# Attention and gated MLP block on one core: program order from the wo stage on, its large GpSimd work on VectorE

## The chip, the core and the metric

The kernel runs on one core of a Trainium2 chip. A core has five queues that work side by side and wait for one another through semaphores: TensorE (PE in the profile, with its weight loads as PEld), VectorE (DVE), ScalarE (ACT), GpSimd (POOL) and SyncE (SP), which here issues nearly all DMAs. The metric is the device time of one execution in microseconds; the time before is the median of 3 runs.

## The reference

One transformer block on x of 2048 tokens by 640, in float32, without learned scales:

```python
# A: 32 heads of 20, each token sees itself and the 255 before it
qkv = layernorm(x) @ wqkv
p = softmax(where(mask, q @ k.T * 20**-0.5, -1e9))
h = x + (p @ v) @ wo
# B: F = 1728, Fh = 864
z = gelu(layernorm(h) @ w_in)
z1, z2 = z[:, :Fh], layernorm(z[:, Fh:])
g = w_sp @ z2 + b_sp[:, None]          # w_sp is 2048 x 2048, over tokens
out = h + (z1 * g) @ w_out
```

## The kernel before

Tokens lie in 16 tiles of 128. Every float32 operand of a large product is split in two parts: hi, a rounded copy (made by ScalarE), and lo, the difference raw - hi (a two-input subtraction). A product is hi x hi + hi x lo + lo x hi, three TensorE instructions. Some products also use a scheme with seven block products in place of eight: the seven left blocks and seven right blocks (B11, T1, T2, B22, T3, B21, T4) are sums and differences of quarters, each with its own hi and lo.

The stages, in order of time:

1. LayerNorm, v and q, k (to about 190 us), then attention (to about 488 us). Attention runs over 130 steps `s`, four heads at a time: in step s, scores of unit u = s, its exponentials on ScalarE, and the product with v (`pv_item`) of unit s - 2. Each odd unit copies half of its output bank to `ot` (on ScalarE or VectorE, line 397) and SyncE stores that to `o_d`; a later pv product in the same bank waits for the copy. The row sums go with it: `inverse_sums(c)` loads them again, takes the reciprocal on VectorE and stores it to `r_d`. It is a generator: each `yield` puts the rest one step later. So is `proj_early`, which in the last 16 steps loads wo and splits it (lines 180 and 181), loads two pairs of token tiles of the output (`load_o`: five DMAs and the reciprocals), multiplies (`norm_o`) and splits (`split_o`) tiles 0 and 1. `proj_o(0)` and `proj_o(1)`, the product with wo, run in the last two steps.
2. The wo stage (to about 583 us): a loop over the 16 tiles. For each: `norm_o` and `split_o` of a later tile, `proj_o` (30 TensorE instructions), h = x + product, store to `h_d`, LayerNorm, transposes (`turn_h`) and a store of the transposed tile to `hn_d`. Beside it, `win1_prep` makes the right blocks of w_in's first half, and the first left blocks of stage 3 are prepared.
3. z1 (to about 668 us): `z_pair`, 8 pairs of tiles, 8 steps each.
4. z2 for 8 tiles (to about 716 us): `z2_pair`, four pairs of tiles. Each is four steps (t, h), a row tile t by a half h: 15 products into a bank (tag `a`, four banks), then a gelu on ScalarE into the row `z[t]`. Then come the statistics of the row (`stat`: two bn_stats and an aggregate on VectorE, three operations of one column on GpSimd), `norm` (scaling on ScalarE), and `right_blocks` of the pair, which the gates use as right operand.
5. `first_gate`, 8 pairs (to about 856 us): products of w_sp with these rows; the partial result goes to `g_d`.
6. z2 for the other 8 tiles (to about 904 us), then `second_gate`: the second half of w_sp, plus g_d, times z1, transposed (`turn_y`) and multiplied by w_out (`project`). In the first of these pairs w_out is loaded tile by tile into two buffers and split (`put_wout`).

From stage 3 on the program is a list `steps`, each a TensorE part and an evacuation, and a table `later`: `at(n, f)` puts f ahead of step n. `run(n)` writes first all of `later[n]`, in the order in which they were put there, then the step's product, then its evacuation:

```python
def run(n):
    for f in later.pop(n, []):
        f()
    if 0 <= n < len(steps):
        steps[n][0]()
        steps[n][1]()
```

Events of a pair are put there when the pair is written, pair after pair. At n0 + 4, the first step of the next pair, stand the older pair's `stat(1, 1)`, `norm(1)` and fourth part of the right blocks, then the new pair's lo of tile t = 1 (at n0 of the new pair).

What sets the order on the queues: up to line 626 `manual_schedule` is in force, which keeps TensorE, VectorE, ScalarE and SyncE in the order in which the program writes its instructions. `ms.close()` there ends it. From then on a scheduler orders the instructions by its own model, with what the program wrote as a start; it can also place later instructions among earlier ones, as it did with three loads of x and one of w_in that SyncE issues at 452 to 456 us. GpSimd is under the scheduler throughout.

Of the kernel before, what the change touches and what calls it, by code (L numbers as in the profile page):

```python
# [15 lines left out]
P = 128  # L16
# [18 lines left out]
def block_kernel(ctx, tc, x, wqk, wv, wo, w_in, wsp, bsp, w_out, out):  # L35
# [45 lines left out]

    def gemm(ps, n, lhs, rhs, ks):
# [61 lines left out]
    def norm_o(i, eng):  # L144
        ot, rs = ots[i]
        eng.tensor_tensor(out=ot, in0=ot, in1=rs[:, None, :].to_broadcast([P, KD, P]), op=OP.mult)

    def split_o(i, eng):
        ot, _ = ots[i]
        osp = mem["osp2"] if i % 3 == 2 else t1((2 * KD + i % 3 * 2) * D, 2, KD, P)  # L150
        if eng is nc.vector:
            eng.tensor_copy(out=osp[:, 0], in_=ot)
        else:
            nc.scalar.activation(osp[:, 0], ot, AF.Copy)
        eng.tensor_tensor(out=osp[:, 1], in0=ot, in1=osp[:, 0].bitcast(F32), op=OP.subtract)
        ots[i] = osp

# [7 lines left out]
    def proj_early():  # L165
# [12 lines left out]
        for k in range(KD):  # L178
# [3 lines left out]
            if k in (1, 3):  # L182
                yield
        yield
        rs = load_o(0)
        yield
        yield
        rs()
        yield
        yield  # L190
        load_o(1)()
        yield
        for i in range(2):
            norm_o(i, nc.vector)
            split_o(i, nc.vector)
            yield


    with ExitStack() as ab:
# [132 lines left out]
        def inverse_sums(c):  # L332
# [8 lines left out]
            yield  # L341
            nc.vector.reciprocal(out=t, in_=t)
# [28 lines left out]
        def pv_item(u):  # L371
# [20 lines left out]
            if kb % 2:  # L392
# [4 lines left out]
                if u >= NU - 5 or j == 0 and u < NU - LEAD:  # L397
# [183 lines left out]
        for s in range(NU + 2):  # L581
# [5 lines left out]
            for hh in range(4):  # L587
# [9 lines left out]
                if hh == 2 + s - NU and s >= NU:  # L597
                    if s == NU:
                        psB.close()
                        psW = pool(psB, "psW", space=PSUM)  # L600
                    pre_ps.append(proj_o(s - NU, psW.tile([P, 2, 512], F32, tag="wo", bufs=3, name=f"wo_ps{s - NU}")))
                if s >= 2:
# [3 lines left out]
                    if hh == 3:  # L606
                        next(pv, None)
            if u1 == NU:
# [17 lines left out]
    ms.close()  # L626
# [78 lines left out]
    def win1_prep(raw):  # L705
        seven, last = win1
        src = w_in[:, :FH].rearrange("k (h c) -> k h c", h=2)
        for k in range(2):
# [5 lines left out]
            for f in right_blocks(lambda: [s[k] for s in seven], *(raw[:, b, h] for b in range(2) for h in range(2)),  # L714
                                  eng=nc.gpsimd):
# [9 lines left out]
    def win2_prep(raw):  # L725
        for k in range(KD):
# [5 lines left out]
            minus(win2[0][:, 1, k], raw, win2[0][:, 0, k].bitcast(F32), nc.gpsimd)  # L732
# [33 lines left out]
    def turn_h(i):  # L766
        ht = mem["ho"][i % 3]
        if i < NT - 2:
# [99 lines left out]
    def z2_pair(q, i, j, k):  # L868
# [6 lines left out]
        def prep(t, first, eng):  # L875
# [3 lines left out]
            else:  # L879
                minus(a[t][:, 1], r3, a[t][:, 0].bitcast(F32), eng)  # L880
# [11 lines left out]
        for t, tile_t in ((0, i), (1, j)):  # L892
# [3 lines left out]
            at(m - (1 if soon else 3), lambda t=t: prep(t, True, None))  # L896
            at(m - (1 if soon else 2), lambda t=t: prep(t, False, nc.gpsimd if t else nc.vector))
# [6 lines left out]
        def stat(t, h):  # L904
# [4 lines left out]
            if h:  # L909
                nc.vector.bn_aggr(out=mv[:, 0:2], in_=st)  # L910
                nc.gpsimd.tensor_scalar(out=mv[:, 2:3], in0=mv[:, 1:2], scalar1=EPS, scalar2=None, op0=OP.add)
                nc.gpsimd.tensor_tensor(out=mv[:, 3:4], in0=mv[:, 2:3], in1=half, op=OP.pow)
                nc.gpsimd.tensor_scalar(out=mv[:, 2:3], in0=mv[:, 0:1], scalar1=mv[:, 3:4], scalar2=-1.0,
                                        op0=OP.mult, op1=OP.mult)

        def norm(t):
            mv = stats[t][1]
            nc.scalar.activation(z[t], z[t], AF.Identity, bias=mv[:, 2:3], scale=mv[:, 3:4])
# [11 lines left out]
    def gate_pair(p, c, post, extra):  # L930
# [13 lines left out]
        eng = nc.vector if p else nc.gpsimd  # L944

# [6 lines left out]
        def s13():  # L952
            plus(s1, a21, a22, eng=eng)
# [267 lines left out]
```

## Time and profile before

| | us |
|---|---|
| median of 3 runs | 1164.73 (1162.14 to 1165.46) |
| the profiled execution | 1165.89 |
| its span, first to last instruction | 1163.7 |
| TensorE busy | 1102.1 |
| VectorE / ScalarE / GpSimd busy | 736.8 / 553.9 / 404.8 |

Times in the profile are microseconds from the span's start. A group of instructions is told by line, engine, operation, the tiles it writes and reads, their shapes and count, then busy time and mean duration of one, then the idle time of the engine just ahead of them and what ended it. `[5.00 <-DVE ot L400]` behind an instruction of the timeline means that its engine was idle for 5.00 us and was released by VectorE's write of `ot` in line 400. SPq is SyncE's queue of DMAs. The lines that carry the argument are shown in the prediction.

### The profile page before, as it was taken

How to read it: one execution, taken by the hardware profiler on the slowest of the kernel's cores; microseconds unless marked ns; L12 is line 12 of the kernel's file. 1: busy time of each engine (PE TensorE's matmuls, PEld its weight loads, DVE VectorE, ACT ScalarE, POOL GpSimd, SP SyncE). 2: the span in 40 equal slices, each digit the busy share in tenths (PEclk: the TensorE clock that was granted, in tenths of full speed). 3: DMA queues.
4: the chain of work that ended last, by engine and by line, in shares of the span. 5: the costliest groups of instructions: out<-in, count | busy, mean ns of one | idle time of the engine just before them, and what ended most of it. 6: DMA issues, size and time to landing. Idle time of an engine off the chain costs nothing.

```text
span 1163.7 us, 28646 instructions
## 1 busy us (share of the span) xinstructions
PE 1102.1 (95%) x11152; PEld 994.7 (85%) x11152; DVE 736.8 (63%) x1961; ACT 553.9 (48%) x1181; POOL 404.8 (35%) x530
## 2 busy tenths in 40 slices
PE   6999999999999999788999998999999799999998
PEld 6998886667877777588999997999999699999998
DVE  5541213788999986679858468655547874655542
ACT  4334433258998889534257566433336531222110
POOL 3124443456666667446421066000117420000000
PEclk9999999999999999889999999999999999999999
DMA  4222355545555543578736512232341454444332
GB/s 149 78 69 80 136 169 201 184 152 176 184 182 176 179 136 125 164 233 270 245 138 210 167 65 73 67 130 87 119 152 39 157 167 152 142 132 143 93 94 68
DMA packets 79800, 165.35 MB, mean 142 GB/s; under 512 B 10752, under 2 KB 43264, under 8 KB 75776
## 3 DMA queue, kind: packets, MB, share of 16 engines
q1 hardware_dynamic: 77360, 158.28, 42.0%
q10 hardware_dynamic: 2304, 5.24, 1.2%
q8 instruction: 87, 1.43, 0.5%
q14 instruction: 49, 0.40, 0.1%
HBM read 108.83 MB, written 54.66 MB: 140 GB/s over the span
## 4 chain that ended last, share of the span: by engine, by line
PE 62%; ACT 8%; issue 7%; POOL 7%; DVE 6%; DMA 6%; SPq 3%; ACTq 0%; POOLq 0%; DVEq 0%
PE g L992 21%; PE out_ps L1057 8%; ACT pt L363 5%; PE pv L386 4%; PE bank L300 3%; PE bank L361 3%; PE zx L835 2%; POOL sg L486 2%; PE zv L835 2%; PE zb L886 2%; PE zy L835 2%; PE zw L835 1%; PE wo_ps L89 1%; PE qk L467 1%; PE qk L468 1%
## 5 line engine op out<-in xcount | busy, mean ns | idle before, releaser
L363 ACT ACTIVATE pt<-bank 128x384 f32<-128x384 f32 (+2 forms) x512 | 202.5, 484 | 29.4 <-PE bank L361 22.3
L992 PE MATMUL g<-zl,aw 128*128 128x432 f32 x768 | 174.4, 363 | 8.8 <-ACT zl L650 8.3
L650 ACT ACTIVATE aw<-fx 128x512 fp32r<-128x512 f32 (+2 forms) x160 | 92.9, 595 | 187.3 <-PE g L992 122.3
L310 DVE CUSTOM_DVE_ANT_0 junk<-bank,strip 128x288 bf16<-128x288 f32 x392 | 156.2, 454 | 15.2 <-PE bank L300 13.8
L992 PEld LDWEIGHTS g<-zl,aw 128*128 128x128 f32 x768 | 145.4, 190 | 17.3 <-ACT zl L650 10.5
L992 PE MATMUL g<-ze,aw 128*128 128x432 f32 x576 | 136.2, 366 | 4.6 <-ACT aw L650 4.5
L386 PE MATMUL pv<-pt,v_sb 128*32 128x192 f32 (+3 forms) x1984 | 130.9, 326 | 10.1 <-DVE ot L400 5.0
L644 DVE TENSOR_TENSOR aw<-fx,aw 128x512 fp32r<-128x512 f32 (+2 forms) x152 | 111.9, 746 | 37.0 <-ACT aw L650 36.3
L992 PEld LDWEIGHTS g<-ze,aw 128*128 128x128 f32 x576 | 109.8, 192 | 10.3 <-ACT aw L650 5.2
L361 PE MATMUL bank<-slot 123*32 123x288 bf16 (+7 forms) x1536 | 110.0, 280 | 2.4 <-issue 1.1
L365 POOL TENSOR_SCALAR_AFFINE_SELECT pt<-pt 128x512 f32<-128x512 f32 x128 | 81.9, 640 | 70.6 <-ACT pt L363 69.3
L1057 PE MATMUL out_ps<-wout,y_sp 128*128 128x320 f32 (+1 forms) x630 | 96.2, 309 | 0.4 <-ACT y_sp L122 0.4
L886 PE MATMUL zb<-win,aw 128*128 128x432 f32 x480 | 95.3, 359 | 0.0
L1057 PEld LDWEIGHTS out_ps<-wout,y_sp 128*128 128x128 f32 (+1 forms) x630 | 94.1, 188 | 1.2 <-ACT y_sp L122 0.7
L886 PEld LDWEIGHTS zb<-win,aw 128*128 128x128 f32 x480 | 89.9, 187 | 4.7
L300 PE MATMUL bank<-slot 120*32 120x288 bf16 (+6 forms) x1280 | 92.2, 277 | 0.9 <-issue 0.8
L483 DVE TENSOR_TENSOR rest<-qk,sg 128x512 f32<-128x512 f32 x40 | 27.7, 692 | 89.5 <-ACT sg L481 89.5
L386 PEld LDWEIGHTS pv<-pt,v_sb 128*32 128x32 f32 x1984 | 61.9, 111 | 17.8 <-issue 14.3
L361 PEld LDWEIGHTS <-slot 123*32 123x32 bf16 x1728 | 60.3, 98 | 17.1 <-issue 8.3
L486 POOL TENSOR_TENSOR sg<-rest,sg 128x512 bf16<-128x512 f32 x40 | 46.5, 1164 | 75.1 <-ACT sg L485 73.2
L368 POOL TENSOR_SCALAR_AFFINE_SELECT pt<-pt 128x512 f32<-128x512 f32 x112 | 71.6, 639 | 0.0
L644 DVE TENSOR_TENSOR row<-g,row 128x432 f32<-128x432 f32 x80 | 48.2, 604 | 36.1 <-PE g L992 32.7
(192 smaller groups left out, 2221.1 us busy)
## 6 DMA issues: line engine op xcount, KB each, us to landing
slot<-qk_d SPq DMA_DIRECT2D x144, 160.0 KB
fx<-wsp_in SPq DMA_DIRECT2D x32, 512.0 KB
qk_d<-sg SPq DMA_DIRECT2D x40, 384.0 KB
fx<-hn_d SPq DMA_DIRECT2D x32, 320.0 KB
o_d<-ot SPq DMA_DIRECT2D x64, 128.0 KB
xb<-qk_d SPq DMA_DIRECT2D x48, 160.0 KB
z_d<-row SPq DMA_DIRECT2D x16, 432.0 KB
g_d<-row SPq DMA_DIRECT2D x16, 432.0 KB
```

Of the source, the lines that this page charges most:

```text
L300: nc.tensor.matmul(ps[32 * j:32 * j + 32, o:o + w], one(st, 120, 0, hh, q0, 32), k, start=True, stop=True, tile_position=(0, 32 * j))
L310: nc.vector.tensor_tensor_reduce(out=junk[:, :n], in0=ps[:, :n], in1=keep, scale=1.0, scalar=NEG, op0=OP.add, op1=OP.max, accum_out=m_cols ...
L361: nc.tensor.matmul(ps[32 * i:32 * i + 32, b + o:b + o + w], one(st, 123, 1, hh, k0, 32), q, start=True, stop=True, tile_position=(0, 32 * i))
L363: nc.scalar.activation(pt[:, hh, :n], ps[:, :n], AF.Exp, scale=SCALE)
L365: nc.gpsimd.affine_select(out=pt[:, :, :P], in_=pt[:, :, :P], pattern=[[0, 4], [1, P]], base=0, channel_multiplier=-1, compare_op=OP.is_ge ...
L386: nc.tensor.matmul(ps[32 * hh:32 * hh + 32, a - 512 * c:b - 512 * c], v_sb[:, kb, v0:v0 + 32], pt[:, hh, a - kb * P:b - kb * P], start=fir ...
L644: (eng or nc.vector).tensor_tensor(out=out, in0=a, in1=b, op=op)
L650: nc.scalar.activation(out, a, AF.Copy)
L835: nc.tensor.matmul(ps, a[x], b[:, y], start=start and m + x + y == 0, stop=stop and m == n - 1 and x == 1, skip_group_check=True)
L886: nc.tensor.matmul(b[0][:, :HF], a[t][:, x, kk], win2[0][:, y, kk, h * HF:(h + 1) * HF], start=kk + x + y == 0, stop=kk == KD - 1 and x == 1)
L992: nc.tensor.matmul(ps, w[m][:, x, k], zc[k][m][:, y], start=start and k + x + y == 0, stop=stop and k == 3 and x == 1, skip_group_check=True)
L1057: nc.tensor.matmul(ps[j][:, :HD], src[:w, a, k, :], e1["wout"][:w, b, k, j * HD:(j + 1) * HD], start=(k == 0 and a + b == 0), stop=(k == K ...
```

## The change

- `ms.close()` is removed, so program order holds to the end for TensorE, VectorE, ScalarE and SyncE.
- Subtractions and sums that went to GpSimd from wo on go to VectorE: split_o's lo, the right blocks of `win1_prep` and of `z2_pair`, win2's lo, the second row tile's lo in `z2_pair`, the preparations of the first pair of either gate, w_out's lo. GpSimd keeps the three one-column operations of each LayerNorm.
- `norm(0)` and the first three parts of the right blocks go from n0 + 2 to n0 + 3.
- The wo loop is written anew, as a pipeline over iterations: in iteration i the product of tile i, `norm_o` and `split_o` of tile i + 1, the sum and the statistics of tile i - 1, its scaling, and the transposes of tile i - 2. LayerNorm's last step moves from VectorE to ScalarE (`scaled`); h_d's store moves from ScalarE's queue to SyncE's. The transposes of tile 14 fall into the loop, that of tile 15 goes to step 2, and what followed it moves one step.
- The end of attention: one split of wo a step where two stood together, `load_o` earlier, the reciprocal one step later, `norm_o(2)` ahead of the loop; the copies of the units 123 to 125 go from ScalarE to VectorE; `proj_o` of the last two steps is written behind the pv of its step.

```diff
+    def stats_of(mv, st):
+        nc.vector.bn_aggr(out=mv[:, 0:2], in_=st)
+        nc.gpsimd.tensor_scalar(out=mv[:, 2:3], in0=mv[:, 1:2], scalar1=EPS, scalar2=None, op0=OP.add)
+        nc.gpsimd.tensor_tensor(out=mv[:, 3:4], in0=mv[:, 2:3], in1=half, op=OP.pow)
+        nc.gpsimd.tensor_scalar(out=mv[:, 2:3], in0=mv[:, 0:1], scalar1=mv[:, 3:4], scalar2=-1.0,
+                                op0=OP.mult, op1=OP.mult)
+
+    def scaled(dst, src, mv):
+        nc.scalar.activation(dst, src, AF.Identity, bias=mv[:, 2:3], scale=mv[:, 3:4])
...
-    def split_o(i, eng):
+    def split_o(i, on_dve=False):
...
-        eng.tensor_tensor(out=osp[:, 1], in0=ot, in1=osp[:, 0].bitcast(F32), op=OP.subtract)
         ots[i] = osp
+        return lambda: nc.vector.tensor_tensor(out=osp[:, 1], in0=ot, in1=osp[:, 0].bitcast(F32), op=OP.subtract)
...
-            if k in (1, 3):
-                yield
+            if k == 2:
+                rs0 = load_o(0)
+            if k == 4:
+                rs1 = load_o(1)
+            yield
+        rs0()
         yield
-        rs = load_o(0)
-        yield
-        yield
-        rs()
-        yield
-        yield
-        load_o(1)()
+        rs1()
         yield
         for i in range(2):
-            norm_o(i, nc.vector)
-            split_o(i, nc.vector)
+            norm_o(i)
+            split_o(i, True)()
             yield
+        norm_o(2)
...
             nc.sync.dma_start(t, rows(o_d[:, DH, c * 512:(c + 1) * 512], 32 * S))
+            yield
             yield
             yield
             nc.vector.reciprocal(out=t, in_=t)
...
-                if u >= NU - 5 or j == 0 and u < NU - LEAD:
+                if u >= NU - 2 or j == 0 and u < NU - LEAD:
...
-    ms.close()
...
-            for f in right_blocks(lambda: [s[k] for s in seven], *(raw[:, b, h] for b in range(2) for h in range(2)),
-                                  eng=nc.gpsimd):
+            for f in right_blocks(lambda: [s[k] for s in seven], *(raw[:, b, h] for b in range(2) for h in range(2))):
...
-            at(m - (1 if soon else 2), lambda t=t: prep(t, False, nc.gpsimd if t else nc.vector))
+            at(m - (1 if soon else 2), lambda t=t: prep(t, False))
...
-        f = right_blocks(lambda: zc[k], *blocks, nc.vector if k == 3 else nc.gpsimd)
+        f = right_blocks(lambda: zc[k], *blocks)
         at(n0 + 1, lambda: stat(0, 0))
-        at(n0 + 2, lambda: (stat(0, 1), norm(0), f[0](), f[1](), f[2]()))
-        at(n0 + 3, lambda: stat(1, 0))
+        at(n0 + 2, lambda: stat(0, 1))
+        at(n0 + 3, lambda: (stat(1, 0), norm(0), f[0](), f[1](), f[2]()))
         at(n0 + 4, lambda: (stat(1, 1), norm(1), f[3]()))
         at(n0 + 5, lambda: (f[4](), f[5](), f[6]()))
...
-        eng = nc.vector if p else nc.gpsimd
...
-                split(e1["wout"][:, 0, k], e1["wout"][:, 1, k], e1["h"][k // 4], nc.gpsimd)
+                split(e1["wout"][:, 0, k], e1["wout"][:, 1, k], e1["h"][k // 4])
...
+    for i in range(1, NT + 1):
+        more = i + 1 < NT
+        if 1 < i < NT:
+            pre_ps.append(proj_o(i, acc_tile(f"wo_ps{i}")))
+        if 1 < i < NT - 1:
+            norm_o(i + 1)
+        if more:
+            lo = split_o(i + 1)
+        if i > 1:
+            add_h(i - 1)
+        if more:
+            lo()
+        if i == 1:
+            add_h(0)
+        if i == 1 or i % 2 == 0 and i + 4 < NT:
             load_o(i // 2 + 2)()
+        for n in (2, 3, 4) if i == 1 else (i + 3,) if i + 3 < NT else ():
             load_x2(n)
+        bn_h(i - 1)
+        next(w1, None)
+        scaled(hn(i - 1), hs.pop(i - 1), stat_h.pop(i - 1)[1])
+        run(i - NT - 1)
         if i > 1:
             turn_h(i - 2)
+        if i % 3 == 1:
             next(w1, None)
```

`add_h(i)` is the sum h = x + product on VectorE and its store; `bn_h(i)` is two bn_stats and `stats_of`.

More of the change, by code (lines that the diff above doesn't have):

```diff
@@ L596, in block_kernel @@
                     next(rows)
[L597 to L601, printed above, removed]
                 if s >= 2:
@@ L607, in block_kernel @@
                         next(pv, None)
+                if hh == 2 + s - NU and s >= NU:
+                    if s == NU:
+                        psB.close()
+                        psW = pool(psB, "psW", space=PSUM)
+                    pre_ps.append(proj_o(s - NU, psW.tile([P, 2, 512], F32, tag="wo", bufs=3, name=f"wo_ps{s - NU}")))
             if u1 == NU:
@@ L731, in win2_prep @@
             yield
[L732 removed]
+            minus(win2[0][:, 1, k], raw, win2[0][:, 0, k].bitcast(F32))
             for _ in range(4):
@@ L873, in z2_pair, with prep @@
         z = [row(), row()]
-        def prep(t, first, eng):
+        def prep(t, first):
             r3 = r[t].rearrange("p (k t) -> p k t", k=KD)
```

63 lines of the change are left out of this document (26 added, 37 removed).

## The prediction

> **What bounds the kernel now.** I read the page first, then the busy time of the engines stage by stage, then TensorE's timeline at each place where it idles, then the queues of the other engines there.
>
> ```profile
> span 1163.7 us, 28646 instructions
> PE 1102.1 (95%) x11152; PEld 994.7 (85%) x11152; DVE 736.8 (63%) x1961; ACT 553.9 (48%) x1181; POOL 404.8 (35%) x530
> 466.00:488.00 22.00, 13.73 (x261) 9.60 (x258) 10.70 (x16) 12.78 (x36) 11.37 (x17) 0.83 0.57 182
> 488.00:583.00 95.00, 86.28 (x569) 83.66 (x569) 80.60 (x132) 30.93 (x55) 49.25 (x52) 0.93 0.72 236
> 583.00:668.00 85.00, 85.00 (x440) 81.22 (x439) 55.03 (x102) 51.61 (x97) 12.68 (x8) 1.00 0.51 176
> 668.00:716.00 48.00, 48.00 (x245) 45.59 (x244) 34.47 (x50) 29.32 (x51) 31.13 (x34) 1.00 0.20 66
> 716.00:734.00 18.00, 13.27 (x51) 11.30 (x50) 14.98 (x28) 12.17 (x23) 6.95 (x10) 0.81 0.14 47
> 904.00:945.00 41.00, 32.42 (x151) 29.49 (x150) 35.14 (x53) 20.61 (x37) 21.24 (x16) 0.92 0.49 166
> ```
>
> Columns of the stages: length; busy time of PE, PEld, DVE, ACT, POOL; granted clock; DMA share; GB/s. TensorE (PE) is the bound. The change can win only its idle time from about 460 us on: 8.3 us at the end of attention (22.00 - 13.73), 8.7 in the wo stage, 4.7 at the entry of the first gates, 8.6 at that of the second, and what the clock loses behind these gaps. The z_pair stage (583 to 668) and the zb products (668 to 716) are at 100%: there is nothing to win there and something to lose.
>
> ```profile
> 471.19 1.08 PE L386 MATMUL pv<-pt,v_sb 128*32 128x256 f32 x8 [5.00 <-DVE ot L400]
> 487.69 5.93 PE L89 MATMUL wo_ps<-t 128*128 128x320 f32 x30 [2.22 <-DVE t L152]
> 498.53 4.56 PE L89 MATMUL wo_ps<-t,osp 128*128 128x320 f32 x30
> 512.27 7.16 PE L89 MATMUL wo_ps<-t 128*128 128x320 f32 x30 [1.55 <-DVE xh L1165]
> 725.51 0.47 PE L992 MATMUL g<-zl,aw 128*128 128x432 f32 x1 [4.40 <-ACT zl L650]
> 729.81 3.08 PE L992 MATMUL g<-ze,aw 128*128 128x432 f32 x8
> 931.25 3.21 PE L992 MATMUL g<-ze,aw 128*128 128x432 f32 x8 [4.49 <-ACT aw L650]
> ```
>
> A gap costs twice: 30 products behind a wait of 2 us take 5.9 to 7.2 us where 4.6 is normal, and 8 gate products take 3.1 us where 0.2 us each is normal. The Trainium skill (TensorE: Matmul & The Clock Gate, Part 1) puts the drop to half clock at about 3.4 us without work; here waits of 1.55 and 2.22 us already lengthen what follows, so the measurement decides.
>
> **The change in the z2 stage, the largest term.** Each pair of rows is four TensorE steps (t,h) of 15 products. Durations:
>
> ```profile
> L886 PE MATMUL zb<-win,aw 128*128 128x432 f32 x237 | 47.1, 359 | 0.0
> L890 ACT ACTIVATE row<-zb 128x432 f32<-128x432 f32 x13 | 6.7, 517 | 1.8 <-PE zb L886 1.8
> L908 DVE BATCH_NORM_STATS2 stz<-row 128x6 f32<-128x432 f32 x13 | 7.7, 590 | 0.6 <-ACT row L890 0.6
> L910 DVE BATCH_NORM_AGGREGATE mvz<-stz 128x2 f32<-128x12 f32 x6 | 1.2, 202 | 0.2
> 723.80 0.22 POOL L911 TENSOR_SCALAR mvz<-mvz 128x1 f32<-128x1 f32 x1
> 724.78 0.27 POOL L913 TENSOR_SCALAR mvz<-mvz 128x1 f32<-128x1 f32 x1
> L918 ACT ACTIVATE row<-row,mvz 128x864 f32<-128x864 f32 x6 | 6.6, 1108 | 9.2 <-POOL mvz L913 9.2
> L650 ACT ACTIVATE zl<-row 128x432 fp32r<-128x432 f32 x6 | 3.2, 558 | 0.3 <-POOL row L644 0.2
> 726.78 1.92 ACT L650 ACTIVATE zl<-row 128x432 fp32r<-128x432 f32 x4 [0.32 <-DVE row L644]
> L650 ACT ACTIVATE aw<-fx 128x640 fp32r<-128x640 f32 x5 | 3.6, 723 | 0.0
> L644 DVE TENSOR_TENSOR zl<-row,zl 128x432 fp32r<-128x432 f32 x7 | 4.0, 604 | 2.9 <-ACT zl L650 2.9
> L644 DVE TENSOR_TENSOR ze<-row,ze 128x432 fp32r<-128x432 f32 x9 | 9.1, 1029 | 3.5 <-ACT ze L650 3.5
> L644 DVE TENSOR_TENSOR aw<-fx,aw 128x640 fp32r<-128x640 f32 x3 | 2.5, 826 | 2.9 <-ACT aw L650 2.9
> ```
>
> In total VectorE gains from the move: a subtraction of 128x432 takes 0.604 us alone and 1.029 while GpSimd works. All of a pair's vector work in the new order is 11 right-block operations x 0.5 (0.604 less the 0.1 by which neighbours overlap: four copies of 0.558 took 1.92), four bn_stats, two aggregates and two "lo" parts of 0.83: about 10.5 us, under TensorE's 60 x 0.199 = 11.9. By sums it fits. But both queues are now written by hand, and they wait for each other. I follow them from the end of one pair's last gelu, gelu(1,1), to that of the next:
>
> - bn_stats, aggregate: 0.9. Three small GpSimd operations: 1.25 (723.80 to 725.05). norm(1), 1.11: ends at 3.4.
> - ScalarE: hi(B21), then hi(T2), which waits for a VectorE difference, then hi(B22); only then gelu(0,0), done at 5.4. VectorE: two differences, then "lo" of the row tile t=1, which was GpSimd's: done at 5.3.
> - VectorE: three lo's and a difference, 7.4. ScalarE: hi(T4), hi of the next tile, gelu(0,1), done at 9.0; gelu(1,0), 9.4.
> - The statistics of row 0 wait for gelu(0,1): 9.9. GpSimd 11.2. norm(0), now behind gelu(1,0): 12.4. hi(B11) 12.9; lo and difference 14.1; hi(T1) 14.7; hi of the next tile 15.3; gelu(1,1) 15.7.
>
> The loop takes 15.7 us for 11.9 us of products (60 x 47.1/237), so the queues lag 3.8 us more per pair. TensorE notices through the "lo" of t=1: its third step waits for it, 5.3 us after the last gelu. The first pair, without a predecessor, ends 1.35 us late, so pair 2 stalls 1.3 us. Pair 3 stalls 4.3 and pair 4 stalls 6.4, because the first gate's preparations (five VectorE operations of 0.6 and four copies of 0.5 in these two loops) stand in the same queues. At the gate, 27 products of three pieces run, then the fourth piece needs B21 of the last row: 5 us behind the last gelu, a stall of 3.0. T2 accumulates in the bank of B11, whose evacuation now stands behind all remaining copies of the last row in ScalarE's queue: 2.5. Sum 17.5, and 1.5 for the clock: 19 us. Today this entry loses 4.7 idle, 2.5 in its window by the clock (19% of 13.27) and some 1.5 after it, say 9. **First z2 stage: +10.** A microsecond more or less in the loop moves the last gelu by three, so the bounds are +14 (a loop of 17 us, while GpSimd's three take longer under VectorE's load) and -5 (no lag: only some 4 us of the entry remain).
>
> Second z2 stage: the same 19, and 2 more, because there the evacuation is VectorE's and stands behind w_out's first lo as well: 21. Today it loses 8.6 idle and 8% of 32.42, 11.2. Six of these are w_out's:
>
> ```profile
> 922.60 4.37 POOL L123 TENSOR_TENSOR wout<-hr,wout 128x640 fp32r<-128x640 f32 x1 [3.87 <-ACT wout L122]
> 929.94 0.74 ACT L122 ACTIVATE wout<-hr 128x640 fp32r<-128x640 f32 x1 [3.39 <-DMA hr<-w_out_in]
> ```
>
> GpSimd holds w_out's buffer for 4.37 us, the next load waits for it on SP, ScalarE waits for the load, and the gate's own copy behind it makes the 4.49 us gap at 931. On VectorE the lo takes 0.83, and that chain goes. 21 - 11.2 = **+10**.
>
> z_pair steps keep their engines; only five win2 copies and lo's of 128x864 (some 0.9 to 1.0 us each, an estimate from the rows of 432 and 640) now fall at fixed places, where they can hold a copy that TensorE's third next step needs: **+1**, bounds 0 and 3.
>
> **End of attention and wo stage.**
>
> ```profile
> 452.70 1.59 SPq L127 DMA_DIRECT2D xh<-x_in  x2
> 464.79 6.82 DMA o_d<-ot
> 477.99 2.44 DMA o_d<-ot
> 472.97 4.28 SPq L134 DMA_DIRECT2D m<-o_d  x5
> 469.89 0.83 DVE L181 TENSOR_TENSOR t<-m,t 128x640 fp32r<-128x640 f32 x1
> 485.06 0.95 DVE L342 RECIPROCAL inv<-inv 128x128 f32<-128x128 f32 x1 [6.07 <-DMA inv<-o_d]
> L73 DVE BATCH_NORM_STATS2 stc<-xh 128x6 f32<-128x320 f32 x30 | 13.1, 478 | 0.2
> L154 ACT ACTIVATE t<-m 128x640 fp32r<-128x640 f32 x9 | 6.6, 730 | 11.5 <-DMA m<-o_d 8.8 <-PE wo_ps L89 2.7
> L650 ACT ACTIVATE ho<-ht_ps 128x640 f32<-128x640 f32 x14 | 9.7, 695 | 18.0 <-PE ht_ps L775 13.6 <-DVE xh L1165 2.8 <-PE wo_ps L89 1.4
> ```
>
> The 5.00 us gap at 466 stems from four wo splits ahead of one pv copy on VectorE; one split a step removes it. Next late are r's rows. SP today sends later loads early (xh at 452.70); without them wo's loads start some 3 us sooner and so does the landing of the sums (464.79 + 6.82). But SP then issues load_o(0) and load_o(1), 3 to 4.3 us each, before r_d's store and r's load: From 468.5 on SP's queue is a load of the sums and a store (1.2), load_o(0) and a store (4), load_o(1) (4), r_d's store (0.6, 2.2 to land), r's load (0.6, 2.2): r is there at about 482 to 483, not at 472 where norm_o(0) stands. VectorE waits, and behind norm_o(0) stand two splits, a reciprocal, norm_o(2) (7 us together) and the pv copy of unit 125, which was ScalarE's; TensorE's pv of unit 126 shares that bank. wo's first product starts at about 489.6 (today 487.69): +2. Then the last reciprocal waits on VectorE for a store and a load ahead of tile 2's lo: +2 more.
>
> In the tile loop lo(i+1) (0.83), bn_stats (2 x 0.48), aggregate, three GpSimd operations (1.25 or somewhat more), the scaling of 640 (an estimate of 0.9, from 1.108 for 864), ho (0.695) and the next hi (0.73) form a ring through three queues: 5.5 to 6.1 us, I take 5.8, against 4.6 + 0.5 of TensorE and (583 - 498.5)/14 = 6.0 today: -2. w_in's load, now issued behind load_o(2) and three x tiles, holds ScalarE ahead of a scaling once: +3. Together **+5**; bounds -9 (TensorE's 5.1 us a tile from a start 2 us later, and no hold by w_in) and +13 (6.3 us a tile).
>
> **Sum:** 5 + 1 + 10 + 10 = +26 on the profiled execution's 1165.9 us (span 1163.7 and 2.2 around it). That one lies 1.2 above the median of the runs, so about 1190.
>
> **Rivals.** (a) *The queues keep up and the change wins.* If no lag builds up, the gate entries lose 4 and 6 us instead of 9 and 11 (-5 each), and the wo stage runs at TensorE's pace (-9); with z_pair's +1 this is -18: 1147. For it: the total of vector work fits, and VectorE's lo's shrink from 1.029 to 0.604. Against: the loop above would have to lose 3.8 us of waits. The Trainium skill (GPSIMD Engine Reference, § 4.1 Engine selection) speaks for it: two-input elementwise work belongs on VectorE, GpSimd being about twice as slow. The trace agrees, with 4.37 us there for w_out's lo against 0.83 for the same size on VectorE. (b) *Only the wo stage wins*, the lag is as forecast: -9 + 1 + 20 = +12, 1177. For it: VectorE is free of GpSimd in a stage where it was 85% busy. (c) *The ring takes 6.3 us a tile and both loops 17 us*: 13 + 1 + 14 + 14 = +42, about 1206. (d) The order is the written one in name only, and nothing much moves; against it, the attention part is under that rule already, and its trace shows four splits ahead of the copy just as written.
>
> **How the numbers follow.** Forecast 0.50 (own range 1182 to 1200), (a) 0.18, (b) 0.18, (c) 0.10, (d) and halves that cancel 0.04. About 0.3% (3.5 us) is what a measurement tells from no change. Faster is (a): 0.18; same 0.04; slower 0.78. The range from 1158 to 1206 leaves out most of (a) and the tail of (c).
>
> **What would show it.** In the z2 stage: TensorE waiting for "aw" (the lo of t=1) at the third step of pairs 2 to 4, growing; gelus 16 us apart per pair. At the gate entries: no large GpSimd work, a wait for "zl" of about 3 us, one for a copy of "g". Near 931: no wait behind w_out. In the wo stage: VectorE idle before norm_o(0), about 5.8 us a tile. I am wrong if zb's products run without gaps.

## The result, and the profile after

The changed kernel takes 1223.67 us (median of 4 runs, 1222.90 to 1226.54) against 1165.10 for the kernel before in the same session: ratio 1.050, 95% interval 1.0453 to 1.0546. It is slower by 5%, where 1190 had been forecast.

The first lines of the page of the kernel after, as they were shown for before (engine, busy us, share of the span, instructions):

```profile
span 1222.5 us, 28561 instructions
PE 1121.0 (92%) x11152; PEld 999.3 (82%) x11152; DVE 737.7 (60%) x2021; ACT 565.8 (46%) x1194; POOL 301.1 (25%) x472
```

GpSimd lost 104 us of work and VectorE gained only 1, for two reasons: the scaling of the wo loop went to ScalarE (16 operations of 0.81 us), and its own subtractions became shorter (128x432 into `ze` 0.60 us, before 0.98). TensorE's busy time rose by 19 us for the same 11152 instructions, which it ran at a lower clock (granted clock 0.973, before 0.984), and some 40 us of idle time came on top. Where the stages begin, from TensorE's timelines of the two profiled executions (us from the span's start; each is the first product of its kind):

| | first wo product | first z1 product | first zb product | second half's first zb | span |
|---|---|---|---|---|---|
| before | 487.69 | 582.44 | 664.79 | 856.11 | 1163.7 |
| after | 494.56 | 603.24 | 692.35 | 895.18 | 1222.5 |
| longer by | 6.9 | 13.9 | 6.8 | 11.5 | 19.7 |

Of the 6.9, 2.2 us stand already at 460, ahead of every changed instruction. Of z1's 6.8, some 3.5 belong to the next column: before, the scheduler put twelve zb products among the last ones of z1, so 18 z1 products (just under 0.2 us each) still came behind the first zb. Put right, z1 lost about 3.3 us and the first z2 stage with its gates about 15.0. No stage became shorter.

The waits of TensorE in the kernel after from 440 us on, grouped (what waited, for whom; total us, times, longest):

```profile
PE zb L894 <- DVE aw L653: 22.1, 6, 5.2
PE pv L396 <- DVE ot L410: 12.4, 1, 12.4
PE g L993 <- DVE row L653: 9.6, 5, 4.6
PE ht_ps L783 <- ACT m L90: 7.7, 7, 3.6
PE wo_ps L99 <- ACT t L164: 6.1, 8, 1.8
```

With the smaller groups they make 74.2 us, where before has 32.2 in its same stretch: 42 of the 59 us lost are new waits; most of the rest is the slower products. Each has its place in the timeline. The end of attention, first VectorE, then TensorE:

```profile
475.64 0.42 DVE L410 COPY ot<-pv 128x256 f32<-128x256 f32 x1 [0.54 <-PE pv L396]
486.42 0.82 DVE L156 TENSOR_TENSOR m<-m 128x640 f32<-128x640 f32 x1 [10.35 <-DMA m<-r_d]
...
493.20 0.41 DVE L410 COPY ot<-pv 128x256 f32<-128x256 f32 x1
```

```profile
493.75 0.87 PE L396 MATMUL pv<-pt,v_sb 128*32 128x192 f32 x8 [12.39 <-DVE ot L410]
494.56 6.77 PE L99 MATMUL wo_ps<-t 128*128 128x320 f32 x30
508.48 4.08 PE L99 MATMUL wo_ps<-t,osp 128*128 128x320 f32 x26 [1.50 <-DVE osp L166]
```

norm_o(0) waits 10.35 us for r's rows, and everything that is written behind it waits too: with it, nine operations stand ahead of the pv copy at 493.20, for which TensorE has been standing 12.39 us. In the wo loop, one quiet iteration on VectorE, GpSimd and ScalarE, and two on TensorE:

```profile
550.66 0.83 DVE L166 TENSOR_TENSOR osp<-m,osp 128x640 fp32r<-128x640 f32 x1 [2.27 <-ACT osp L164]
...
552.75 0.40 POOL L84 TENSOR_SCALAR mvc<-mvc 128x1 f32<-128x1 f32 x1 [4.30 <-DVE mvc L83]
...
554.63 0.92 ACT L90 ACTIVATE m<-xh,mvc 128x640 f32<-128x640 f32 x1 [4.00 <-POOL mvc L86]
555.46 0.68 ACT L659 ACTIVATE ho<-ht_ps 128x640 f32<-128x640 f32 x1
556.04 0.72 ACT L164 ACTIVATE t<-m 128x640 fp32r<-128x640 f32 x1
```

```profile
550.68 4.94 PE L99 MATMUL wo_ps<-t,osp 128*128 128x320 f32 x30 [0.45 <-ACT osp L164]
556.82 4.93 PE L99 MATMUL wo_ps<-t 128*128 128x320 f32 x30 [0.45 <-ACT t L164]
562.97 4.95 PE L99 MATMUL wo_ps<-t 128*128 128x320 f32 x30 [0.45 <-ACT t L164]
```

A tile takes 6.15 us. The wait on TensorE is only 0.45, so its own row hides the cause; the other rows tell it. VectorE's lo waits for ScalarE's hi, the statistics stand behind that lo, ScalarE is 4.00 us idle for them, then come scaling, `ho` and the next hi one behind the other, and that hi releases TensorE and the next lo. The first z2 stage and the entry of the first gates:

```profile
711.89 12.10 PE L894 MATMUL zb<-win,aw 128*128 128x432 f32 x60 [1.24 <-DVE aw L653]
728.97 14.73 PE L894 MATMUL zb<-win,aw 128*128 128x432 f32 x60 [4.98 <-DVE aw L653]
748.15 7.36 PE L894 MATMUL zb<-win,aw 128*128 128x432 f32 x28 [4.44 <-DVE aw L653]
763.30 0.46 PE L993 MATMUL g<-zl,aw 128*128 128x432 f32 x1 [1.33 <-ACT zl L659]
764.38 0.67 PE L993 MATMUL g<-zl,aw 128*128 128x432 f32 x2 [0.62 <-DVE zl L653]
767.47 2.53 PE L993 MATMUL g<-ze,aw 128*128 128x432 f32 x6 [2.42 <-ACT row L659]
```

ScalarE's waits in that stretch (692 to 755), grouped:

```profile
ACT row L90 <- POOL mvz L86: 11.3, 5, 2.5
ACT row L898 <- PE zb L894: 6.7, 4, 2.4
ACT zl L659 <- DVE row L653: 5.6, 3, 3.4
ACT ze L659 <- DVE row L653: 4.1, 3, 1.4
```

ScalarE, which must also evacuate TensorE's banks (the gelus), stands 11.3 us at `norm` for GpSimd's statistics and 9.7 at the blocks for VectorE's differences. Only 6.7 us did it wait for TensorE, as an engine that keeps up would. The second half shows the same waits for aw and, at its gate entry, waits for g's sums that stand late in VectorE's queue.

### The profile page after: what moved, and what is told of

Same layout as the page of the kernel before. It is cut to its first block, busy times and chain, and to the rows that moved or that the text cites. A ratio compares the mean times of both kernels' runs of the same rounds, so it can differ in the third digit from the quotient of the medians.

```text
span 1222.5 us, 28561 instructions
## 1 busy us (share of the span) xinstructions
PE 1121.0 (92%) x11152; PEld 999.3 (82%) x11152; DVE 737.7 (60%) x2021; ACT 565.8 (46%) x1194; POOL 301.1 (25%) x472
## 4 chain that ended last, share of the span: by engine, by line
PE 38%; DVE 10%; ACT 6%; DMA 3%; POOL 2%; issue 2%; SPq 1%; DVEq 0%; POOLq 0%; ACTq 0%
PE g L993 20%; PE out_ps L1058 8%; PE zx L843 2%; PE zv L843 2%; DVE row L653 2%; ACT row L90 1%; PE zb L894 1%; PE zy L843 1%; DVE zl L653 1%; DVE aw L653 1%; PE zw L843 1%; PE wo_ps L99 1%; SPq L144 1%; DVE stz L916 1%; PE yt_ps L1047 1%
## 5 line engine op out<-in xcount | busy, mean ns | idle before, releaser
L993 PE MATMUL g<-zl,aw 128*128 128x432 f32 x768 | 171.8, 362 | 3.0 <-ACT zl L659 1.8
L894 PE MATMUL zb<-win,aw 128*128 128x432 f32 x480 | 105.4, 383 | 22.1 <-DVE aw L653 22.1
L993 PEld LDWEIGHTS g<-ze,aw 128*128 128x128 f32 x576 | 108.7, 193 | 18.9 <-DVE row L653 6.6
L894 PEld LDWEIGHTS zb<-win,aw 128*128 128x128 f32 x480 | 97.0, 204 | 30.1 <-DVE aw L653 24.3
L653 DVE TENSOR_TENSOR aw<-fx,aw 128x512 fp32r<-128x512 f32 (+2 forms) x160 | 100.6, 643 | 31.7 <-ACT aw L659 31.5
L375 POOL TENSOR_SCALAR_AFFINE_SELECT pt<-pt 128x512 f32<-128x512 f32 x128 | 84.3, 659 | 62.7 <-ACT pt L373 61.1
L309 PE MATMUL bank<-slot 120*32 120x288 bf16 (+6 forms) x1280 | 94.5, 278 | 1.5 <-issue 1.3
L1058 PE MATMUL out_ps<-wout,y_sp 128*128 128x320 f32 (+1 forms) x630 | 95.3, 310 | 0.4 <-ACT y_sp L132 0.4
L84 POOL TENSOR_SCALAR mvz<-mvz 128x1 f32<-128x1 f32 x16 | 6.1, 382 | 336.5 <-DVE mvz L83 336.5
L378 POOL TENSOR_SCALAR_AFFINE_SELECT pt<-pt 128x512 f32<-128x512 f32 x112 | 72.6, 648 | 0.0
```

Of the source, the lines that this page charges most:

```text
L309: nc.tensor.matmul(ps[32 * j:32 * j + 32, o:o + w], one(st, 120, 0, hh, q0, 32), k, start=True, stop=True, tile_position=(0, 32 * j))
L375: nc.gpsimd.affine_select(out=pt[:, :, :P], in_=pt[:, :, :P], pattern=[[0, 4], [1, P]], base=0, channel_multiplier=-1, compare_op=OP.is_ge ...
L653: (eng or nc.vector).tensor_tensor(out=out, in0=a, in1=b, op=op)
L894: nc.tensor.matmul(b[0][:, :HF], a[t][:, x, kk], win2[0][:, y, kk, h * HF:(h + 1) * HF], start=kk + x + y == 0, stop=kk == KD - 1 and x == 1)
L993: nc.tensor.matmul(ps, w[m][:, x, k], zc[k][m][:, y], start=start and k + x + y == 0, stop=stop and k == 3 and x == 1, skip_group_check=True)
L1058: nc.tensor.matmul(ps[j][:, :HD], src[:w, a, k, :], e1["wout"][:w, b, k, j * HD:(j + 1) * HD], start=(k == 0 and a + b == 0), stop=(k == K ...
```

## The experiments

The theory was that the written order makes the loss: queues that run in order wait for one another in rings. Rival: VectorE has too much to do. Times are medians, each with its ratio to the kernel before on the same chip.

**1. Order or engine.** First the scheduler again from the wo loop on, with all else as changed:

```diff
+    ms.close()
     psK = ctx.enter_context(ExitStack())
```

> The changed kernel with ms.close() put back ahead of the wo loop: the scheduler orders from there on; work, engines and the end of attention stay as changed. Theory (the loss lies in the written order of queues that wait for one another, not in VectorE's extra work): of the 13.7 + 3.9 + 14.4 + 19.9 us lost behind attention most comes back and only attention's 4.6 stays: 1160 to 1180. Rival (VectorE now has too much to do): the scheduler cannot make it less, it stays above 1205.

1152.69 us, ratio 0.9913 (0.9885 to 0.9941). One line gives back the whole loss and more, though the end of attention stayed as bad (pv stood 13.0 us for ot there). Then the kernel before with the engines alone changed (three of its edits):

```diff
-            split_o(i + 1, nc.gpsimd)
+            split_o(i + 1, None)
...
-        f = right_blocks(lambda: zc[k], *blocks, nc.vector if k == 3 else nc.gpsimd)
+        f = right_blocks(lambda: zc[k], *blocks)
...
-        eng = nc.vector if p else nc.gpsimd
+        eng = nc.vector
```

> The kernel before, the scheduler still ordering from the wo loop on, with only the engine of the large GpSimd work changed to VectorE (wo's lo, the right blocks, win2's lo, the lo of row tile 1, the first gate pairs' preparations, w_out's lo). Theory: the move by itself costs nothing and may gain some (a subtraction of 128x432 takes 0.60 us there alone, 1.03 beside GpSimd): 1150 to 1172. Rival (the move is the loss): above 1190.

1146.19 us, ratio 0.9843 (0.9803 to 0.9883): the move alone is a gain of 1.6%. The gate products that read `zl`, in before and in this kernel, from the pages (count, busy us, mean ns, idle time ahead of them):

```profile
L992 PE MATMUL g<-zl,aw 128*128 128x432 f32 x768 | 174.4, 363 | 8.8 <-ACT zl L650 8.3
```

```profile
L991 PE MATMUL g<-zl,aw 128*128 128x432 f32 x768 | 170.8, 359 | 1.3 <-ACT zl L650 1.1
```

They lose 7.5 us less in waits, and their busy time is 3.6 less for the same count. In before's trace GpSimd's subtractions `row` and `zl` stand in the chain that led to these entries. The fourth corner is the changed kernel with the large work back on GpSimd (two of its edits):

```diff
-            for f in right_blocks(lambda: [s[k] for s in seven], ...):
+            for f in right_blocks(lambda: [s[k] for s in seven], ..., nc.gpsimd):
...
-        f = right_blocks(lambda: zc[k], *blocks)
+        f = right_blocks(lambda: zc[k], *blocks, None if k == 3 else nc.gpsimd)
```

> The changed kernel in its program order, with the same large operations given back to GpSimd (the other half of the two-by-two with the move alone). Theory: the order is the loss, so this is no faster than the changed kernel: the rings now run through GpSimd's slower subtractions (4.4 us for 128x640 against 0.83), 1223 to 1260. Rival (VectorE's load is the loss): below 1190.

1221.62 us, ratio 1.0498 (1.0462 to 1.0534):

| ratio to before | large work on GpSimd | on VectorE |
|---|---|---|
| scheduler from the wo loop on | 1 (before) | 0.9843 |
| program order | 1.0498 | 1.0500 (after) |

In program order the engine makes no difference to the total; the order does. "No faster" held, but the reason I gave was half wrong, for two differences cancel. In this kernel's timeline the first z1 product stands at 587.61 behind a wo stage of 94.5 us, 14 less than in the changed kernel: the statistics no longer stand behind a lo on VectorE that waits for ScalarE's hi, which opens the ring shown above (w_in's blocks moved too, and the two were not tried apart). It gives 12.6 us back later: in z1 (93.4 us against 89.1), from the first zb to the second half (207.5 against 202.8) and behind it (330.9 against 327.3). So in the wo loop the moved lo is part of the ring that program order makes.

**2. Which part of the order: the z2 stage.** The first try put the scalings and blocks one step later:

```diff
-        at(n0 + 3, lambda: (stat(1, 0), norm(0), f[0](), f[1](), f[2]()))
-        at(n0 + 4, lambda: (stat(1, 1), norm(1), f[3]()))
-        at(n0 + 5, lambda: (f[4](), f[5](), f[6]()))
+        d = 0 if k == 3 else 1
+        at(n0 + 3, lambda: stat(1, 0))
+        at(n0 + 3 + d, lambda: (norm(0), f[0](), f[1](), f[2]()))
+        at(n0 + 4, lambda: stat(1, 1))
+        at(n0 + 4 + d, lambda: (norm(1), f[3]()))
+        at(n0 + 5 + d, lambda: (f[4](), f[5](), f[6]()))
```

> The changed kernel with norm(0) and the first three parts of the right blocks one step later, norm(1) and the other parts too, for the first three pairs of each z2 stage; the statistics stay. Nothing is taken away, only what stands behind what changes. Theory (a loop gelu - statistics - GpSimd's three - norm - copy - next gelu, longer than a pair's 11.9 us of products, makes the lag): the scaling no longer waits in ScalarE's queue ahead of the next gelu, the waits of 1.2, 5.0 and 4.4 us (and 1.2, 5.0, 5.2) for aw fall below 2 in all, and some 14 to 18 us a stage less the later gate entry come back: 1190 to 1208. Rival (ScalarE and VectorE have simply more work than a pair's products cover): under 5 us gained, above 1218.

1219.66 us, ratio 1.0483 (1.0446 to 1.0519): a miss, not told apart from the changed kernel. Waits for aw fell from 22.1 to 12.8, and waits for zl at the gates rose from 1.8 to 8.4. Its flaw is in the edit: within step n0 + 4, `stat(1, 1)` is now written behind row 0's scaling and blocks, so row 1's statistics start only when these are through (in its trace row 0's scaling runs at 721.59, row 1's at 728.81, after 3.21 us of waiting for them); one ring was exchanged for another. The second try moved only what TensorE was seen to wait for, row tile 1's two parts:

```diff
-            at(m - (1 if soon else 3), lambda t=t: prep(t, True))
-            at(m - (1 if soon else 2), lambda t=t: prep(t, False))
+            at(m - (1 if soon else 3 + t), lambda t=t: prep(t, True))
+            at(m - (1 if soon else 2 + t), lambda t=t: prep(t, False))
```

> The changed kernel with both parts of row tile 1 one step earlier in each z2 pair (hi and lo ahead of the older pair's norm(1) and its blocks). Theory (the lag is made by the whole loop through ScalarE's and VectorE's queues; TensorE only shows it at aw): the waits for aw fall from 22 to under 8, but the gate entries then wait longer for zl and for g's copies, 3 to 6 us less in all, about 1219. Rival (the lo behind the older pair's work is by itself the cause): 18 to 24 us less, about 1202.

1222.54 us, ratio 1.0508 (1.0466 to 1.0549): nothing gained, not even the 3 to 6 that I expected. The largest of TensorE's grouped waits at zb and g in this kernel:

```profile
PE g L993 <- ACT zl L659: 9.1, 6, 3.3
PE g L993 <- DVE row L653: 8.6, 5, 4.2
PE zb L894 <- ACT aw L659: 7.9, 2, 4.0
PE zb L894 <- DVE aw L653: 4.6, 4, 2.2
```

The 22.1 us for VectorE's aw became 4.6 for it, 7.9 for ScalarE's copy of the same tile, and 7.3 more for zl at the gates. The lag stayed and took other names. The third try wrote the stage anew, for the first three pairs, together with the earlier tile 1:

```diff
+            at(n0 + 3, lambda: stat(1, 0))
+            at(n0 + 4, lambda: (stat(1, 1), norm(0), f[0]()))
+            at(n0 + 5, lambda: (f[1](), f[2](), norm(1)))
+            at(n0 + 6, lambda: (f[3](), f[4]()))
+            at(n0 + 7, lambda: (f[5](), f[6]()))
```

> The changed kernel with the z2 stage written in another order, for the first three pairs of each stage: the statistics of row 1 ahead of the scaling of row 0, each scaling one step or more behind its statistics, the blocks spread over four steps, and row tile 1 a step earlier. The last pair is unchanged. Theory (ScalarE and VectorE have room, only the order makes them wait for each other): waits for aw under 4 us in all and 12 to 20 us less than the changed kernel, 1204 to 1212; the gate entries keep their waits because the last pair's work is where it was. Rival (program order cannot keep this stage at TensorE's pace, since the two queues together are too full): under 5 us less, above 1218.

1195.98 us, ratio 1.0286 (1.0251 to 1.0321): 0.0214 less than the changed kernel's ratio, about 25 us and more than expected. The zb products of the kernel after and of this one, from the pages, and ScalarE's two largest waits in this one from 692 to 740:

```profile
L894 PE MATMUL zb<-win,aw 128*128 128x432 f32 x480 | 105.4, 383 | 22.1 <-DVE aw L653 22.1
```

```profile
L894 PE MATMUL zb<-win,aw 128*128 128x432 f32 x480 | 95.5, 359 | 0.7 <-DVE aw L653 0.7
```

```profile
ACT row L898 <- PE zb L894: 8.9, 7, 2.5
ACT row L90 <- POOL mvz L86: 2.3, 2, 2.0
```

ScalarE now waits for TensorE, the right way round, and the products take 359 ns instead of 383: 10 us of clock besides the waits. The gate entry's waits stayed, 3.30 us for zl and 2.05 for a copy of g. Two more runs split this edit; both diffs are against the kernel just shown. Without the earlier tile 1:

```diff
-            at(m - (1 if soon else 3 + t), lambda t=t: prep(t, True))
-            at(m - (1 if soon else 2 + t), lambda t=t: prep(t, False))
+            at(m - (1 if soon else 3), lambda t=t: prep(t, True))
+            at(m - (1 if soon else 2), lambda t=t: prep(t, False))
```

> The changed kernel with the other order of the z2 stage, but row tile 1's two parts back at their old step. Theory (the statistics and scalings tie the loop; the lo is one part of it, since it stands behind the older pair's blocks): most of the gain stays, 1196 to 1206, with waits for aw of 2 to 8 us in all. Rival (the early lo does it once the scalings are out of its way): the gain falls to under 8 us, above 1214.

1196.83 us, ratio 1.0288 (1.0250 to 1.0327), with 1.4 us of waits for aw: the whole gain stays. And with the earlier tile 1 and the statistics first, but the blocks not spread:

```diff
-            at(n0 + 4, lambda: (stat(1, 1), norm(0), f[0]()))
-            at(n0 + 5, lambda: (f[1](), f[2](), norm(1)))
-            at(n0 + 6, lambda: (f[3](), f[4]()))
-            at(n0 + 7, lambda: (f[5](), f[6]()))
+            at(n0 + 4, lambda: (stat(1, 1), norm(0), f[0](), f[1](), f[2]()))
+            at(n0 + 5, lambda: (norm(1), f[3]()))
+            at(n0 + 6, lambda: (f[4](), f[5](), f[6]()))
```

> The changed kernel with row tile 1 a step earlier, the statistics of row 1 ahead of the scaling of row 0 and both scalings one step later, but the blocks not spread: each part stands behind its scaling as in the changed kernel, one step later. Theory (the order of statistics and scalings ties the loop): 1196 to 1204, waits for aw under 5 us. Rival (the blocks' copies and differences, each waiting for the other engine, fill the queue ahead of the next gelu unless they are spread): above 1212.

1207.16 us, ratio 1.0368 (1.0325 to 1.0410), with 5.3 us of waits for aw; between the two theories. From the changed kernel's 1.050, statistics ahead of a later scaling gives about 1.3%, the spread of the blocks another 0.8%, the lo by itself nothing. What TensorE was seen to wait for was not what had to be moved.

**3. The wo loop.** The scaling of a tile goes one iteration later:

```diff
         if i > 1:
+            scaled(hn(i - 2), hs.pop(i - 2), stat_h.pop(i - 2)[1])
             add_h(i - 1)
...
-        scaled(hn(i - 1), hs.pop(i - 1), stat_h.pop(i - 1)[1])
         run(i - NT - 1)
...
+    scaled(hn(NT - 1), hs.pop(NT - 1), stat_h.pop(NT - 1)[1])
```

> The changed kernel with one thing moved in the wo loop: the scaling of tile i - 1 goes one iteration later (ahead of the sum of the next tile), so its statistics have a whole iteration. Theory (a ring lo - statistics - GpSimd's three - scaling - transposed copy - next hi of 6.15 us a tile sets the pace): a tile takes 5.1 to 5.5 us in quiet iterations and the stage 8 to 12 us less, about 1213. Rival (the pace is set by w_in's preparation on ScalarE and VectorE): under 3 us less.

1208.42 us, ratio 1.0379 (1.0339 to 1.0419): 1.2%, some 14 us. TensorE in this loop:

```profile
545.20 4.64 PE L99 MATMUL wo_ps<-t,osp 128*128 128x320 f32 x30
549.68 0.71 PE L783 MATMUL ht_ps<-ident,m 128*128 128x128 f32 x5
550.14 4.65 PE L99 MATMUL wo_ps<-t 128*128 128x320 f32 x30
```

A tile takes 4.94 us, without a wait, and the stage 94.2 us against 108.7. w_in's preparation was as it had been, so it did not set the pace.

**4. Two waits seen in the trace, removed one at a time.** First the copies of units 123 to 125 go back to ScalarE:

```diff
-                if u >= NU - 2 or j == 0 and u < NU - LEAD:
+                if u >= NU - 5 or j == 0 and u < NU - LEAD:
```

> The changed kernel with the pv copies of units 123 to 125 back on ScalarE. Theory: TensorE's wait of 12.4 us for ot at the end of attention is a copy held on VectorE behind norm_o(0), which waits for r's rows; without it pv of the last units runs on, the wait goes, and wo's first product waits for r's rows instead: 4 to 6 us less than the changed kernel, about 1218. Rival (wo's first product hangs on r's rows alone): within 1.5 us of the changed kernel, with the wait only renamed.

1216.98 us, ratio 1.0473 (1.0436 to 1.0510). The interval overlaps that of the changed kernel, so the gain of 3 to 7 us is not settled by the times; the trace has the mechanism:

```profile
477.32 0.53 PE L396 MATMUL pv<-pt,v_sb 128*32 128x192 f32 x8 [0.61 <-ACT ot L408]
484.17 6.03 PE L99 MATMUL wo_ps<-t 128*128 128x320 f32 x30 [6.32 <-DVE t L162]
```

The wait of 12.39 became 0.61, and wo's first product now waits for norm_o's tile itself. Then w_in's first loads ahead of the wo loop:

```diff
+    next(w1)
     for i in range(1, NT + 1):
```

> The changed kernel with w_in's first loads issued ahead of the wo loop, so ahead of load_o(2) and the three tiles of x. Theory (ScalarE stands 7.20 us at 520.90 for that load, and the scaling behind it holds TensorE for 3.64): that wait goes, 3 to 5 us less than the changed kernel, about 1219. Rival (the load only changes places with load_o(2), whose tile is then late): within 2 us of it.

1228.26 us, ratio 1.0557 (1.0517 to 1.0596): no gain. ScalarE's 7.20 us for the load are gone, yet TensorE's stage takes 107.3 us against 108.7: as I read it, the ring sets the pace behind it, and a wait taken out of a ring-bound loop turns up at another place in it (TensorE: 1.98 us for the sum in `xh`).

**5. Together, and what beats both.** The edits of 4, 3 and the whole z2 edit at once, still in program order:

> The changed kernel with four edits at once, still in program order to the end: copies of units 123 to 125 on ScalarE, w_in's load first, the scaling of the wo loop one iteration later, the z2 stage in the other order. If the single gains (about 6, 4, 15 and 27 us) stand in different places and add up: 1166 to 1178. Rival (each edit only uncovers the next wait): above 1185. What should be left are the waits at the gate entries, 6 us at the first and 12 at the second, and r's rows.

1171.52 us, ratio 1.0061 (1.0039 to 1.0083). The single gains (1.0500 less 0.0027, 0.0121 and 0.0214) would give 1.014, and w_in's load alone nothing; here it may count, because the ring no longer hides it: the transposes' longest wait is 2.0 us, where the kernel with the later scaling alone had 4.6 behind that load. What is left, the four largest of TensorE's grouped waits from 440 us on:

```profile
PE g L1000 <- DVE row L653: 9.8, 6, 4.2
PE g L1000 <- ACT zl L659: 6.6, 2, 3.3
PE wo_ps L99 <- DVE t L162: 6.4, 1, 6.4
PE ht_ps L783 <- ACT m L90: 6.3, 5, 2.0
```

The same with `ms.close()` ahead of the steps of z1, so that the scheduler orders what follows the wo loop:

> The four edits together, and the scheduler takes over behind the wo loop. Theory: what is left of program order's loss lies at the gate entries and in z1, and the scheduler fills these by mixing stages: 1140 to 1152. Rival (the written order of the wo stage, now mended, costs what the scheduler would not): above 1155.

1151.93 us, ratio 0.9901 (0.9864 to 0.9938). From the first zb product to the second half's it takes 183.4 us (189.5 with the order written out), from there to the end 301.5 (313.0). The gates' waits fell from 19.4 us with the order written out to 4.4. The scheduler mixes the stages at their borders (zb products among the last of z1 and among the last of the first gates); that this fills the entries was not tried by itself. Last, the kernel with only the engines changed, and wo's splits one a step:

```diff
-            if k in (1, 3):
-                yield
-        yield
-        rs = load_o(0)
-        yield
-        yield
+            if k == 3:
+                rs = load_o(0)
+            yield
```

> The kernel before with the large GpSimd work on VectorE (scheduler on from the wo stage), and wo's splits one a step instead of two, everything else of attention's end where it was before. Theory: the wait of 5.2 us of pv for a copy at 473, behind four splits on VectorE, goes and wo's first product starts 3 to 5 us sooner: 1141 to 1144. Rival (wo's first product hangs on r's rows all the same): within 1.5 us of 1146.

1145.34 us, ratio 0.9840 (0.9809 to 0.9872), not told apart from 0.9843: the rival was right. pv's longest wait fell from 5.20 to 3.44 us, and a new one of 1.14 stood sooner, at 469. These two kernels, 0.9840 and 0.9843, are the fastest of all the runs.

## Why the prediction was right or wrong

The sign was right, and so were the places of the waits; the size was not: +26 was forecast, +58.6 came, above the top of the range. Four of the prediction's terms failed in size: the tile loop ("5.8 us a tile", -2, and about +13 came), the clock behind the waits ("1.5 for the clock" in each z2 stage, and 7 to 9 came), the evacuations at the second gate entry (2.5 and 2 counted, 8.6 came), and the date of r's rows.

- **First z2 stage, +10; about +15 came.** The waits came where they were put and nearly as long: third step of pairs 2, 3 and 4, 1.24, 4.98 and 4.44 us against 1.3, 4.3 and 6.4; at the gate 1.33 + 0.62 for zl and 2.42 for the copy of g against 3.0 and 2.5. What failed is "1.5 for the clock": behind these waits the products of zb took 4.7 us more than 0.199 each, and those of the gate some 2.3. Over both stages zb was busy 105.4 us, before 95.3. The loop of 15.7 us measured 17.1, 19.1 and 16.4 from last gelu to last gelu (at 705.93, 723.02, 742.12, 758.54), the first of these at the prediction's upper bound of 17. That pair 4's wait was shorter than forecast is no better reading: the slow products ahead of it took up part of the same lag.
- **Second z2 stage, +10; +19.7 came.** w_out's wait did go, as said. But waits of 4.59, 1.68 and 2.32 us for g's sums, behind VectorE's late queue, are 8.6 us where 2.5 and 2 had been counted, two of the pairs' waits were 4.95 and 5.22, and the slow products of zb cost 5 again, with some 4 at the gate.
- **The tile loop, "5.8 us a tile", -2.** The ring that was named is the one that the later scaling broke. Quiet iterations take 6.15: GpSimd's three operations last 1.85 us there (552.75 to 554.60) where 1.25 was counted. All iterations take 6.9 on average. 14 tiles at 0.9 more than before are the 13 us that were lost where 2 were to be won (the 3.64 us of the next point are among them). This is the largest mis-sized term, and rival (c)'s 6.3 was nearer.
- **"w_in's load holds ScalarE once, +3".** The hold was there (7.20 us) and cost TensorE 3.64 once, but taking it away alone won nothing: inside a ring it is no term of a sum.
- **End of attention, +2; +4.6 came.** The copy behind norm_o(0) was named, the price not, because norm_o(0) started at 486.4 and r's rows were not there at 482 to 483. The load of the sums was issued at 471.01, not at 468.5: wo's loads started 1.4 us sooner than before (459.35 against 460.75) and not 3. So r_d's store went out at 481.03 and r's rows landed 3 to 4 us later than counted.
- **z_pair, +1; about +3.3 came,** of which 2.2 us are a wait for the transposed copy `ho` of the last tile at its start.
- **Rival (a)** priced -18 for a kernel whose queues keep up. The move to VectorE under the scheduler came to -16.5 (1162.73 to 1146.19). That is another kernel, with before's wo loop, so the near match is in part luck; the changed kernel under the scheduler came to -10.0, with its bad end of attention. What the prediction held against (a), the waits of the loop, is what happened in program order.
- **The range** was too narrow term by term: the upper bounds of 13, 3, 14 and 14 add up to 44, and the measured 18.5, 3.3, 15.0 and 19.7 lie each above its own. Behind the attention one cause lay under all of them, in-order queues that wait for each other: handing the order back to the scheduler took these losses away together.

## What to carry to other kernels

When an order is written out by hand for several queues, follow for each loop the ring of waits, and put what waits (a scaling, a copy) at least one step behind what it waits for and behind the evacuations that it would hold up. The wait that TensorE shows is often not the place to mend: look at the queue in front of it and ask for whom *that* engine stood idle. And before a move between engines is judged, try it with the order left alone.

## What the runs showed of the hardware

How long must a single wait be before the products behind it run slower? The stages of zb have dense products on both sides of a wait. Two rows stand above for the kernel after (1.24 and 4.98 us); these four are from the kernel with the scalings one step later (start, us, count, wait):

```profile
720.51 6.20 PE L894 MATMUL zb<-win,aw 128*128 128x432 f32 x30 [2.56 <-DVE aw L653]
...
737.46 14.39 PE L894 MATMUL zb<-win,aw 128*128 128x432 f32 x58 [3.84 <-DVE aw L653]
...
921.12 13.54 PE L894 MATMUL zb<-win,aw 128*128 128x432 f32 x60 [2.60 <-DVE aw L653]
937.71 13.44 PE L894 MATMUL zb<-win,aw 128*128 128x432 f32 x58 [3.05 <-DVE aw L653]
```

At 0.199 us each, 30, 58 and 60 products take 6.0, 11.5 and 11.9 us. So the wait of 1.24 us cost 0.2 more, and those of 3.84 and 4.98 cost 2.9 and 2.8. In between the rows part: 2.56 us cost 0.2, but 2.60 cost 1.6 and 3.05 cost 1.9. The granted clock says the same: 1.00 from 720.5 to 726.7, 0.88 from 921.1 to 934.7. The Trainium skill (TensorE: Matmul & The Clock Gate, Part 1) states a drop at about 3.4 us; here shorter waits were already followed by slow products, though not always, and the measurement decides. The prediction said so from two rows of before's wo products (1.55 and 2.22 us), but each of these stands behind an earlier gap with little work between (1.95 us, then five transposes; 0.61 us, then eight pv products), so they were no single waits.

GpSimd's three operations on one column took 1.25 us in before's trace (723.80 to 725.05), and up to 2.65 in the changed wo loop:

```profile
539.66 0.40 POOL L84 TENSOR_SCALAR mvc<-mvc 128x1 f32<-128x1 f32 x1 [5.65 <-DVE mvc L83]
540.14 0.78 POOL L85 TENSOR_TENSOR mvc<-mvc,half 128x1 f32<-128x1 f32 x1
541.02 1.29 POOL L86 TENSOR_SCALAR mvc<-mvc 128x1 f32<-128x1 f32 x1
```

The same third operation takes 0.27 us in the next tiles. What lengthens it was not tried.
